# Interleaving GpSimd's loads with its copies for the later head pairs of a pooled-attention and feed-forward kernel

## The chip, the cores and the metric

The kernel runs on one core of one Trainium2 chip. The metric is device time in microseconds (us) of one execution. The profile comes from one further execution with the hardware profiler on.

The engines are named as the profile names them: PE is TensorE (matrix products; PEld is its weight load), DVE is VectorE, ACT is ScalarE, POOL is GpSimd, SP is SyncE. Each engine takes its instructions in the order in which they were written. SP only issues DMAs; POOL issues DMAs and also computes. All DMAs share 16 DMA engines.

## The reference

```
q_pool = mean of neighbouring query rows (1152 -> 576 rows)
attn   = softmax(q_pool @ k^T / sqrt(64))      # 8 batches x 8 heads
x      = (attn @ v), heads side by side         # 4608 x 512
out    = ((x @ w1) * (x @ w2)) @ w3 @ w_out     # 512 -> 1024 -> 1024 -> 512
```

Inputs and output are float32; products are made in 16-bit floats with 32-bit sums. The kernel folds `w3 @ w_out` into one matrix `T16` and leaves the maximum out of the softmax.

## The kernel before

**Tiling.** Two heads of a batch make a pair; there are `NP` = 32 pairs (four to a batch). A pair has 9 key tiles by 576 pooled query rows for each head. Scores are written in chunks of 512 columns for both heads at once, 10.125 chunks to a pair, 324 in all. For a chunk, PE writes scores to PSUM (L294, tile `psc`), ACT takes the exponential into a ring in SBUF (L300, `er`), and after a pair's last chunk two bursts of products with the values follow (`attend`, L312 and L321, `po`). DVE divides by the row sums (`xn`), and SP transposes the result by DMA into `xT` (L348), for every fourth remainder also `xR` (L330). When a batch is complete, its feed-forward products follow: `pg` (L514, against w1 and w2), the gate `gT` on DVE, `pp` (L535, against `T16`), and a store by SP.

**Order.** The main loop walks the chunks. A planner holds clocks of what PE, ACT and DVE would take and fills the time between chunks with products of earlier batches; whatever it emits stands in that order on PE for good. Preparation of a pair depends on `at`, the position in pairs (chunk times 512 over 5184), and does not enter the planner's clocks.

**Preparing pairs 9 to 31.** Pairs 0 to 8 are transposed on PE (`prep_pe`, queue `prep`). From `NPE` = 9 on, POOL copies the keys from their staging tile `kst` to `kc` (L161), adds neighbouring query rows from `qst` into `qp` (L143), and copies the values from `vst` into one of four tiles `vt` (L152). SP then transposes `kc` into `kT` (L166) and `qp` into `qT` (L172) by DMA. `prep_dma(P)` is called about 1.9 pairs ahead of pair P's scores and emits the three POOL operations at once. The SP parts are entries of the list `turns`, due 1.45 pairs (`turn_k`) and 1.2 pairs (`turn_q`) ahead. Behind the key transpose, `turn_k` puts a one-element copy `seen` on POOL (L168) that reads `kT`: POOL waits there until the transpose has landed. Only then come the loads from HBM of a pair five further on: keys L116, queries L108, and the values of pair P+4 (L123).

So POOL's cycle for a pair is: `seen`, three DMA issues, `kc`, `qp`, `vt`, and a wait at the next `seen`. SP's order for the same stretch mixes `kT` and `qT` with the transposes into `xT` and `xR` and the stores of finished rows (L600).

The buffers that matter: `kst` and `vst` have 5 each, `qst` 3 (each of two pairs, one in either half of the partitions), `kc` 2, `qp` 2 (each of two pairs), `kT` and `qT` 3, `vt` 4.

Of the kernel before, what the change touches and what calls it, by code (L numbers as in the profile page):

```python
# [8 lines left out]
FP16 = mybir.dt.float16  # L9
# [6 lines left out]
NJ = 9  # L16
# [7 lines left out]
def kernel(  # L24
# [11 lines left out]
    nc = tc.nc  # L36
    B, H, S, D = q.shape
# [5 lines left out]
    NP = B * H // 2  # L43
    SCL = 16.0
    NPE = 9
# [5 lines left out]
    ab = ctx.enter_context(tc.tile_pool(name="ab", bufs=4))  # L51
# [25 lines left out]
    kst, vst, qst, kT, qT, qps = {}, {}, {}, {}, {}, {}  # L77
# [25 lines left out]
    def load_q(P):  # L103
        if P % 2 == 0:
            qst[P // 2] = stage.tile([128, 2, 18, D], FP16, tag="qst", bufs=3, name="qst")
        b, h0 = P // 4, 2 * (P % 4)
        o = 64 * (P % 2)
        nc.gpsimd.dma_start(  # L108
            out=qst[P // 2][o:o + 64].rearrange("p u t d -> p u (t d)"),
            in_=q[b, h0:h0 + 2].rearrange("u (p t) d -> p u (t d)", t=18))  # L110

    def load_k(P):
        b, h0 = P // 4, 2 * (P % 4)
        kst[P] = stage.tile([128, 2, NJ, D], FP16, tag="kst", bufs=5, name="kst")
        for js in ((0, 3), (3, NJ)) if P == 0 else ((0, NJ),):
            nc.gpsimd.dma_start(  # L116
                out=kst[P][:, :, js[0]:js[1], :],
                in_=k[b, h0:h0 + 2].rearrange("u (p j) d -> p u j d", j=NJ)[:, :, js[0]:js[1], :])

    def load_v(P):  # L120
        b, h0 = P // 4, 2 * (P % 4)
        vst[P] = stage.tile([128, 2, NJ, D], FP16, tag="vst", bufs=5, name="vst")
        nc.gpsimd.dma_start(  # L123
            out=vst[P].rearrange("p u j d -> p u (j d)"),
            in_=v[b, h0:h0 + 2].rearrange("u (p j) d -> p u (j d)", j=NJ))

    def load(P):


        if P < NP:  # L130
            load_k(P)
            load_q(P)
        if P <= NP:
            load_v(P - 1)

    def pool_q(P, eng=None):

        pp, o = P // 2, 64 * (P % 2)
        if P % 2 == 0:
            qps[pp] = ab.tile([128, NJ, 2, D], FP16, tag="qp", bufs=2, name="qp")  # L140
        r = slice(o, o + 64)
        src = qst[pp][r].rearrange("p u (c two) d -> p u c two d", two=2)
        (eng or nc.vector).tensor_tensor(  # L143
            out=qps[pp][r].rearrange("p c u d -> p u c d"),
            in0=src[:, :, :, 0, :], in1=src[:, :, :, 1, :], op=ALU.add)

    def new_kq(P):
        kT[P] = ab.tile([128, NJ, 128], FP16, tag="kT", bufs=3, name="kT")
        qT[P] = ab.tile([128, NJ, 64], FP16, tag="qT", bufs=3, name="qT")

    def copy_v(P, eng=None):
        (eng or nc.vector).tensor_copy(out=vts[P % 4][:, :, :, 0:D], in_=vst.pop(P))  # L152

    turns = []

    def prep_dma(P):

        pp, o = P // 2, 64 * (P % 2)
        new_kq(P)
        kc = ab.tile([128, NJ, 2, D], FP16, tag="kc", bufs=2, name="kc")  # L160
        nc.gpsimd.tensor_copy(out=kc.rearrange("p j u d -> p u j d"), in_=kst.pop(P))  # L161
        pool_q(P, nc.gpsimd)
        copy_v(P, nc.gpsimd)

        def turn_k():
            nc.sync.dma_start_transpose(out=kT[P], in_=kc.rearrange("p j u d -> p (j u d)"))  # L166
            if P + 5 <= NP:
                nc.gpsimd.tensor_copy(out=seen[:, 0:1], in_=kT[P][0:1, 0, 0:1])  # L168
                load(P + 5)

        def turn_q():
            nc.sync.dma_start_transpose(  # L172
                out=qT[P], in_=qps[pp][o:o + 64].rearrange("p c u d -> p (c u d)"))
        turns.extend([(P - 1.45, turn_k), (P - 1.2, turn_q)])

    kcs, kc_done = {}, {}
# [126 lines left out]
    def attend(P, u):  # L303

        n = take()
        po = bank("po", n)
        for j in range(NJ):
            for i in range(4):  # L310
                r = ((P * NJ + j) * SQ) % RING + 128 * i
                nc.tensor.matmul(  # L312
                    po[:, VW * i:VW * i + D + 1], er[:, u, r:r + 128],
                    vts[P % 4][:, u, j, 0:D + 1],
                    start=(j == 0 and i == 0), stop=(j == NJ - 1 and i == 3),
                    skip_group_check=True)
        if u == 0:
            for j in range(NJ):
                r = ((P * NJ + j) * SQ) % RING + 512
                for s in range(2):  # L320
                    nc.tensor.matmul(  # L321
                        po[64 * s:64 * s + 64, 4 * VW:4 * VW + D + 1], er[:, s, r:r + 64],
                        vts[P % 4][:, s, j, 0:D + 1], start=False, stop=(j == NJ - 1),
                        skip_group_check=True)
        at = max(clock[0], clock[1], exp_done[last_chunk(P)] + T_SEM) + T_PV[u]
        clock[:] = [at] * 2
        give(n, normalize(P, u, po, 5 - u, at))
        b, hp = divmod(P, 4)
        if u == 0 and b % 2 == 1:
            nc.sync.dma_start_transpose(  # L330
                out=xR[:, hp, b // 2].rearrange("p u r -> p (u r)"),
                in_=rems[:, hp].rearrange("p s d -> p (s d)"))
        if u == 0 and hp == 3:
            ended.append((b, [vec + (8.0 if b < 2 else 6.5)]))
# [68 lines left out]
    def swap_due():  # L403
        half = 0 if swaps[0] else 1
        free = 3 if prep[0] or prep[1] else 2
        return bool(swaps[half]) and max(clock) > WEIGHTS[half] and len(spare) >= free and (
            spare[0][0] < min(clock))
# [29 lines left out]
    prep, ffn = ([], []), ([], [])  # L437
# [164 lines left out]
    def last_rows(places, lhsT):  # L602
# [24 lines left out]
        out=ident, in_=ident, compare_op=ALU.not_equal, fill=1.0,  # L627
# [49 lines left out]
    while c < NCHUNK or bursts or ffn[0] or ffn[1]:  # L677
        h = 0 if clock[0] <= clock[1] else 1
        if bursts and (c > bursts[0][0] or c == NCHUNK) and spare and spare[0][0] < clock[h] and (
                fresh or c > bursts[0][0] + 1 or c == NCHUNK):  # L680
            attend(*bursts.pop(0)[1:])
            fresh = False
            while swap_due():
                swap_halves()
            continue
        if c >= NCHUNK or due(c) > clock[h]:
            fresh = False
            if c >= NCHUNK and not tail and not bursts:
                tail = True
                spare += [(max(clock), 4), (max(clock), 5)]  # L690
            keep = 1 if prep[0] or prep[1] or bursts and c > bursts[0][0] - 1 else 0
            if not step(h):
                if swap_due():
                    clock[:] = [max(clock) + 0.1] * 2
                    swap_halves()
                    clock[:] = [clock[0] + 0.1] * 2
                else:
                    clock[h] += 0.02
            while ended and not early and not prep[0] and not prep[1]:
                b, ready = ended.pop(0)  # L700
                add_batch(b, ready)
            continue
        at = c * CH / PAIR
        scores(c, h)
        fresh = True
        for i in range(2):
            clock[i] += T_SC
        expo(c)
        exp_done.append(max(exp_done[-1] if c else 0.0, max(clock) + T_SEM) + T_EXP)
        if c == 0:  # L710
            prep_rest(rest)
        if jobs:
            n, job = jobs.pop(0)
            job()
            vector(n, 0.0)
        if staged < NPE and at >= STAGE.get(
                staged, staged - (0.95 if staged < 4 else 1.3)):
            prep_stage(staged)
            staged += 1
        while events and at >= events[0][0]:  # L720
            _, n, act = events.pop(0)
            act(n)
        todo = prepped < NP and at >= PREP.get(prepped, prepped - (
            0.65 if prepped < 4 else 0.9 if prepped < NPE else 1.9))
        if todo and prepped >= NPE:
            prep_dma(prepped)
            prepped += 1
        elif todo and prepped < staged and prepped in kcs:
            prep_pe(prepped)
            prepped += 1  # L730
        elif early and c >= early[0][0] and len(w3T) < 4:
            w3_transpose(early.pop(0)[1])
        while turns and at >= turns[0][0]:
            turns.pop(0)[1]()
        c += 1
    for emit, store, _, _ in last[:-1]:
# [36 lines left out]
```

## Time and profile before

| what | value |
|---|---|
| time, three runs | 420.18 us median (420.1, 420.18, 423.63) |
| the profiled execution | 425.27 us, of it span 423.3 us |
| granted clock of PE, mean | 0.995 |
| PE busy | 403.7 us (95%) |
| ACT busy | 331.1 us (78%) |
| DVE busy | 218.9 us (52%) |
| POOL busy | 191.2 us (45%) |
| DMA | 59.02 MB in 94219 packets |

The span runs from the first to the last instruction; 1.97 us of the profiled execution lie around it. PE's first product starts 6.0 us into the span and its last ends 3.9 us before the end. In rows of the timeline, the columns are start, duration (both us), engine, line, operation, output and inputs, shape, count, and in brackets the idle time before with what ended it. "issue" in that place stands for a wait on nothing that the profile shows.

### The profile page before, as it was taken

Reading aid. Unit: us, or ns where it says so; the run is one execution under the profiler, and the core shown is the slowest. Engines: PE = TensorE matmul, PEld = TensorE weight load, DVE = VectorE, ACT = ScalarE, POOL = GpSimd, SP = SyncE. Lnnn points to the kernel's source line nnn. Section 1 sums busy time; section 2 is a strip of 40 time slices with the busy share of each in tenths; the row PEclk is TensorE's granted clock in tenths of the full one; section 3 lists DMA queues with packets and bytes.
Section 4 is the critical chain, followed back from the end, with each engine's and each line's share of the span. In section 5 each row is a group of like instructions: output and inputs, shape, how many; then the busy total and the mean of one; then the engine's idle time right before and its main releaser. Section 6 shows DMA issues by size and latency. Waiting matters only on the chain.

```text
span 423.3 us, 17431 instructions
## 1 busy us (share of the span) xinstructions
PE 403.7 (95%) x7666; PEld 318.0 (75%) x7666; DVE 218.9 (52%) x596; ACT 331.1 (78%) x382; POOL 191.2 (45%) x209
## 2 busy tenths in 40 slices
PE   3799999998999999999999899999999999999996
PEld 1366665777768887888788786788878887888993
DVE  2266656875435653565365663356446644542540
ACT  3968888887788888888888788889888888834432
POOL 8233345860566576555655556665569300000000
PEclk9999999999899999999999999999999999999999
DMA  8999999999699999999999999999996215102004
GB/s 120 206 207 202 186 205 204 189 161 121 110 154 206 152 141 153 196 144 121 192 170 132 139 134 132 190 185 150 137 170 141 42 35 133 43 19 101 4 11 141
DMA packets 94219, 59.02 MB, mean 139 GB/s; under 512 B 64832, under 2 KB 84544, under 8 KB 94144
## 3 DMA queue, kind: packets, MB, share of 16 engines
q0 software_dynamic: 26528, 33.56, 50.7%
q1 hardware_dynamic: 67456, 24.22, 35.1%
q8 instruction: 60, 0.98, 1.0%
q10 hardware_dynamic: 160, 0.13, 0.1%
q14 instruction: 15, 0.12, 0.1%
HBM read 67.11 MB, written 9.44 MB: 181 GB/s over the span
## 4 chain that ended last, share of the span: by engine, by line
PE 93%; ACT 3%; issue 2%; DMA 1%; DVE 0%; POOL 0%; DVEq 0%; ACTq 0%; POOLq 0%
PE pg L514 30%; PE psc L294 19%; PE po L312 18%; PE pp L535 15%; PE pT L477 4%; PE po L321 3%; ACT er L300 3%; PE t L262 1%; PE sw L391 1%; DMA kst<-in_k_dram 1%; PE w3t L465 0%; PE pp L608 0%; PE tb L195 0%; POOL qst L108 0%; ACT kc L207 0%
## 5 line engine op out<-in xcount | busy, mean ns | idle before, releaser
L300 ACT ACTIVATE er<-psc 128x1024 f16<-128x1024 f32 x324 | 308.8, 1030 | 52.0 <-PE psc L294 48.7
L294 PE MATMUL psc<-qT,kT 64*128 64x384 f16 (+7 forms) x1152 | 132.3, 291 | 4.6 <-ACT er L300 3.8
L514 PE MATMUL pg<-xT,w2sb 64*128 64x256 f16 x1024 | 131.3, 270 | 0.0
L514 PE MATMUL pg<-xT,w1sb 64*128 64x256 f16 x1024 | 130.7, 271 | 0.1
L514 PEld LDWEIGHTS <-w1sb 64*128 64x128 f16 x1280 | 97.9, 94 | 10.9 <-issue 2.7
L514 PEld LDWEIGHTS <-w2sb 64*128 64x128 f16 x1280 | 96.7, 94 | 6.2 <-issue 0.4
L535 PE MATMUL pp<-T,gT 64*128 64x512 f16 (+1 forms) x552 | 94.4, 376 | 0.0
L312 PEld LDWEIGHTS <-er 128*128 128x128 f16 x2304 | 74.5, 98 | 17.6 <-issue 15.0
L294 PEld LDWEIGHTS <-kT 64*128 64x128 f16 x1152 | 60.6, 95 | 32.5 <-issue 16.8
L312 PE MATMUL po<-vt,er 128*128 128x65 f16 x2304 | 82.4, 194 | 2.0 <-issue 1.8
L506 DVE TENSOR_TENSOR gT<-pg,asb 128x256 f16<-128x256 f32 (+1 forms) x160 | 66.3, 417 | 20.8 <-ACT asb L494 16.3
L497 DVE COPY asb<-pg 128x256 f32<-128x256 f32 (+1 forms) x119 | 48.0, 404 | 32.1 <-PE pg L514 30.5
L340 DVE RECIPROCAL rz<-po 128x4 f32<-128x4 f32 x64 | 12.1, 189 | 89.7 <-PE po L312 46.0
L143 POOL TENSOR_TENSOR qp<-qst 64x1152 f16<-64x1152 f16 x23 | 54.5, 2370 | 1.0
L535 PEld LDWEIGHTS <-gT 64*128 64x128 f16 (+1 forms) x552 | 41.3, 94 | 13.8 <-issue 0.4
L168 POOL COPY seen<-kT 1x1 f16<-1x1 f16 x19 | 3.4, 180 | 88.0 <-DMA kT<-kc 88.0
L152 POOL COPY vt<-vst 128x1152 f16<-128x1152 f16 x28 | 32.1, 1150 | 4.6 <-issue 3.9
L123 POOL DMA_DIRECT2D vst<-in_v_dram x32 | 23.3, 729 | 17.2 <-DMA kst<-in_k_dram 7.4
L116 POOL DMA_DIRECT2D kst<-in_k_dram x33 | 24.0, 729 | 11.7 <-issue 3.0
L343 DVE TENSOR_TENSOR xn<-po,rz 128x256 f16<-128x256 f32 x64 | 27.2, 424 | 2.2
L494 ACT COPY asb<-pg 128x256 f32<-128x256 f32 (+1 forms) x41 | 12.8, 332 | 19.4 <-PE pg L514 18.9
L161 POOL COPY kc<-kst 128x1152 f16<-128x1152 f16 x23 | 26.9, 1169 | 0.0
(62 smaller groups left out, 256.2 us busy)
## 6 DMA issues: line engine op xcount, KB each, us to landing
qst<-in_q_dram POOLq DMA_DIRECT2D x32, 288.0 KB, 6.0
vst<-in_v_dram POOLq DMA_DIRECT2D x32, 288.0 KB, 8.2
kst<-in_k_dram POOLq DMA_DIRECT2D x31, 288.0 KB, 5.4
out_dram<-osb SPq DMA_DIRECT2D x32, 256.0 KB, 3.2
w3h<-in_moe_w_dram POOLq DMA_DIRECT2D x4, 512.0 KB, 15.6
wosb<-in_moe_w_out_dram POOLq DMA_DIRECT2D x1, 1024.0 KB, 13.8
xT<-xn SPq DMA_TRANSPOSE x64, 5.8
w1sb<-in_moe_w_dram POOLq DMA_DIRECT2D x2, 512.0 KB, 15.9
```

The lines of the kernel that those rows point to most:

```text
L116: nc.gpsimd.dma_start(out=kst[P][:, :, js[0]:js[1], :], in_=k[b, h0:h0 + 2].rearrange("u (p j) d -> p u j d", j=NJ)[:, :, js[0]:js[1], :])
L143: (eng or nc.vector).tensor_tensor(out=qps[pp][r].rearrange("p c u d -> p u c d"), in0=src[:, :, :, 0, :], in1=src[:, :, :, 1, :], op=ALU.add)
L152: (eng or nc.vector).tensor_copy(out=vts[P % 4][:, :, :, 0:D], in_=vst.pop(P))
L161: nc.gpsimd.tensor_copy(out=kc.rearrange("p j u d -> p u j d"), in_=kst.pop(P))
L294: nc.tensor.matmul(t[:, u, o:o + ln], kT[P][s, j, :], qv[s, f0:f0 + ln], start=True, stop=True)
L300: nc.scalar.activation(out=er[:, :, r:r + CH], in_=psc.pop(c), func=AF.Exp, bias=0.0, scale=SCALE)
L312: nc.tensor.matmul(po[:, VW * i:VW * i + D + 1], er[:, u, r:r + 128], vts[P % 4][:, u, j, 0:D + 1], start=(j == 0 and i == 0), stop=(j == ...
L343: nc.vector.tensor_tensor(out=xn, in0=acc[:, 0:4, 0:D], in1=rz[:, 0:4].to_broadcast([128, 4, D]), op=ALU.mult)
L497: nc.vector.tensor_copy(out=a, in_=t[:, 0:n])
L506: nc.vector.tensor_mul(out=g, in0=b, in1=a)
L514: nc.tensor.matmul(t[:, n * w:n * w + n], (w1sb, w2sb)[w][s, (m + h) % 2, m // 2, fs], x(s, m), start=start, stop=stop, skip_group_check=True)
L535: nc.tensor.matmul(t, gT[h][s, i, cs], T16[s, i, :], start=start, stop=stop, skip_group_check=True)
```

## The change

`prep_dma` no longer emits POOL's three operations together. A new function `copy_k` makes the key copy. `turn_k(P)` now emits, in this order: the SP transpose of pair P's keys, `seen`, the key load of P+5, the key copy of P+1, the query load of P+5, the query sums of P+1, the value load of P+4, and the value copy of P. Only for the first such pair (P = 9) do key copy and query sums stay in `prep_dma`. The buffers `kT` and `qT` are taken in `turn_k`. Turns now also wait until the planner's queue `prep` of PE transposes is empty.

```diff
-    def prep_dma(P):
-
-        pp, o = P // 2, 64 * (P % 2)
-        new_kq(P)
+    def copy_k(P):
         kc = ab.tile([128, NJ, 2, D], FP16, tag="kc", bufs=2, name="kc")
         nc.gpsimd.tensor_copy(out=kc.rearrange("p j u d -> p u j d"), in_=kst.pop(P))
-        pool_q(P, nc.gpsimd)
-        copy_v(P, nc.gpsimd)
+        kcs[P] = kc
+
+    def prep_dma(P):
 
         def turn_k():
-            nc.sync.dma_start_transpose(out=kT[P], in_=kc.rearrange("p j u d -> p (j u d)"))
+            new_kq(P)
+            nc.sync.dma_start_transpose(
+                out=kT[P], in_=kcs.pop(P).rearrange("p j u d -> p (j u d)"))
             if P + 5 <= NP:
                 nc.gpsimd.tensor_copy(out=seen[:, 0:1], in_=kT[P][0:1, 0, 0:1])
-                load(P + 5)
+            if P + 5 < NP:
+                load_k(P + 5)
+            if P + 1 < NP:
+                copy_k(P + 1)
+            if P + 5 < NP:
+                load_q(P + 5)
+            if P + 1 < NP:
+                pool_q(P + 1, nc.gpsimd)
+            if P + 5 <= NP:
+                load_v(P + 4)
+            copy_v(P, nc.gpsimd)
 
         def turn_q():
+            pp, o = P // 2, 64 * (P % 2)
             nc.sync.dma_start_transpose(
                 out=qT[P], in_=qps[pp][o:o + 64].rearrange("p c u d -> p (c u d)"))
+        if P == NPE:
+            copy_k(P)
+            pool_q(P, nc.gpsimd)
...
-        while turns and at >= turns[0][0]:
+        while turns and at >= turns[0][0] and not prep[0] and not prep[1]:
             turns.pop(0)[1]()
```

## The prediction

> **What bounds the kernel.** I read the page first (busy shares, then the chain that ended last), then the waits, then the rows of PE where it stands idle, then POOL's and SP's rows of one pair.
>
> ```profile
> PE 403.7 (95%) x7666; PEld 318.0 (75%) x7666; DVE 218.9 (52%) x596; ACT 331.1 (78%) x382; POOL 191.2 (45%) x209
> q8 instruction: 60, 0.98, 1.0%
> PE 93%; ACT 3%; issue 2%; DMA 1%; DVE 0%; POOL 0%; DVEq 0%; ACTq 0%; POOLq 0%
> ```
>
> PE is busy for 95% of the span and carries 93% of the chain; POOL, the engine that the change reorders, carries none of it. PE's idle time is 19.6 us: 6.0 before its first product, 3.9 behind its last, and 9.7 between. Pair 9, the first that the change touches, is prepared from about 90 us on, and 4.3 of those 9.7 lie before 25 us. After 90 us, PE's idle stretches over 0.3 us are three, all put down to "issue". The largest, in PE's timeline:
>
> ```profile
> 101.29 0.42 PE L312 MATMUL po<-vt,er 128*128 128x65 f16 x8
> 103.52 1.02 PE L312 MATMUL po<-vt,er 128*128 128x65 f16 x28 [1.81 <-issue]
> ```
>
> It stops in the middle of a burst whose inputs are there. The others are 0.68 us ending at 230.27 and 1.45 us ending at 242.09; a fourth delay, 0.53 us at 252.8, is seen only as a late start. What they share is a distance. The instruction queue (q8 above) moved 60 packets of 0.98/60 MB = 16 KB, and 2 x 7666 PE and PEld instructions over 60 are 256 a packet. Windows laid between the restarts (columns: window, its length, then each engine's busy time and count):
>
> ```profile
> 230.28:242.08 11.80, 10.36 (x256) 8.95 (x256) 6.54 (x21) 9.55 (x11) 6.91 (x7) 1.00 1.03 125
> 242.10:252.80 10.70, 10.44 (x256) 9.16 (x256) 6.73 (x22) 8.11 (x9) 6.80 (x7) 1.00 1.00 130
> ```
>
> 256 products and 256 weight loads are 512 instructions, exactly two packets; from 103.52 to 230.27 it is 4864, nineteen. PE runs dry at the edge of a block of its own instructions, because the next block's packet came late. The packets of that queue start up to 4.1 us after PE crosses the edge before: under 0.7 us where no load runs any more (after 322 us), 3 to 4 us where the DMA engines are full. This is the only door by which the change can reach PE's time.
>
> A stall can cost more than itself. After the one at 103.5 (columns as above, clock third from the end):
>
> ```profile
> 104.00:105.00 1.00, 1.00 (x26) 0.83 (x24) 0.38 (x2) 0.03 (x1) 0.18 (x1) 0.91 0.85 186
> 105.00:108.00 3.00, 3.00 (x32) 2.10 (x28) 1.10 (x3) 2.03 (x3) 2.96 (x4) 0.50 0.46 52
> ```
>
> Three and a half us at half clock lose about 1.8 us, so that stall cost 1.8 + 1.8 = 3.6 us. The stalls of 0.68 and 1.45 us cost no clock. The runs shown differ by 423.63 - 420.1 = 3.5 us, the same size: I take it that a run either has this event or not.
>
> **The change on POOL.** One cycle before, from POOL's timeline:
>
> ```profile
> 219.25 0.18 POOL L168 COPY seen<-kT 1x1 f16<-1x1 f16 x1 [4.75 <-DMA kT<-kc]
> 219.50 0.74 POOL L116 DMA_DIRECT2D kst<-in_k_dram  x1
> 220.23 0.61 POOL L108 DMA_DIRECT2D qst<-in_q_dram  x1
> 220.82 0.73 POOL L123 DMA_DIRECT2D vst<-in_v_dram  x1
> 221.54 1.18 POOL L161 COPY kc<-kst 128x1152 f16<-128x1152 f16 x1
> 222.65 2.39 POOL L143 TENSOR_TENSOR qp<-qst 64x1152 f16<-64x1152 f16 x1
> 224.97 1.15 POOL L152 COPY vt<-vst 128x1152 f16<-128x1152 f16 x1
> ```
>
> The work is the same seven instructions, 7.0 us a pair, none added: the cycle only becomes seen, k, kc, q, qp, v, vt. Counted from `seen`: the key copy ends at 0.25 + 0.74 + 1.18 = 2.2 us, not 3.5 (1.3 earlier); the query load issues at 2.2, not 1.0; the query sums end at 5.2, not 5.8; the value load issues at 5.2, not 1.6; the value copy ends at 7.0 as before, but is that of pair P, not P+1. The whole fits: POOL waits 88 us at `seen` over 19 pairs, 4.6 us each.
>
> **On SP.** `kT` waits for `kc`, and everything behind it on SP waits along:
>
> ```profile
> SPq L166 <- POOL kc L161: 20.9, 8, 4.9
> ```
>
> (total, times, longest) and in SP's timeline:
>
> ```profile
> 222.74 1.94 SPq L166 DMA_TRANSPOSE kT<-kc  x1
> 224.77 1.52 SPq L348 DMA_TRANSPOSE xT<-xn  x1
> 226.38 1.69 SPq L172 DMA_TRANSPOSE qT<-qp  x1
> ```
>
> Here `kT` of pair 20 was due on SP when the chunk of 220.0 us was written, and started when the copy ended, 222.7. Behind it stood `xT`, whose `xn` was ready at 222.2. From `seen` to the next `seen` is 11.4 us here: 3.5 to `kT`'s issue and 7.9 until it lands, because the three loads fill the DMA engines from 221 to 227 (their queue's packets take a share of about 1.0, the transposes' queue moves nothing from 221 to 225). With 1.3 us less the cycle is near 10.1 us, below the 10.85 us that PE takes for a plain pair, so the lag does not pile up, and `kT`, `xT` and `qT` go up to 2.7 us earlier in pairs 11 to 13, 19 to 21 and 26 to 28.
>
> What does PE gain from that? Nothing directly. Each `kT` already lands 3.0 to 11.5 us before the first score product that reads it, each `qT` 1.2 (pair 25) to 9.1 us; no wait of PE names either. An `xT` is first read 0.8 us (fourth batch, landing 206.0, read 206.8) to 28 us after its batch's last one lands. **Sum on the path: 0.** If that cover went, each pair would cost PE what it is late.
>
> The other edits: `vt` of pair P now ends about 7 us after `seen(P)`, near the start of P's scores; the products that read it start over a pair (10.85 us) later: 0. Taking `kT` later (at 1.45 instead of 1.9 pairs) changes nothing, as the pair whose buffer it takes had its last scores at 2.0: 0. The empty-queue condition can hold only pair 9's turn: PE's last transposes (L262) run until 97.1 us and that turn's chunk is at 96.7, so one chunk, 1.1 us, and SP reaches that `kT` only at 99.7, behind `xR`; it lands 9.6 us early: 0.
>
> **What is left: the instruction packets.** Stalls after 104 us are 0.68 + 1.45 + 0.53 = 2.66 us, in the stretch 217 to 253 where the short products of the remainder rows make PE cross a block in 5 to 7 us. The three packets behind them waited 3.1, 3.3 and 3.4 us while `kT`, `xT` and `qT` ran together. Packets that met a load burst waited as long (3.7 us at 165.9, 3.9 at 267.7), but in longer blocks, without a stall. The stall at 101.7 stands before the first moved load (105.0): unchanged. So the change parts the loads, which cost nothing now, and moves the transposes, which do, by 1 to 2.7 us, which may help or hurt. Bounds: all three go, -2.66; or one grows to the size of that at 101.7, clock included, +3.6. I take the smallest of the three gone, -0.5, as the shift is small against the 7 us of a transpose. The profiled execution becomes 425.27 - 0.5 = 424.8; against the median, which is 5.1 lower (3.6 for the event at 101.7, the rest smaller stalls without the profiler, I suppose), 420.18 - 0.5 = **419.7 us**.
>
> [...]
>
> **Rivals.**
> - *All three stalls go*, because spread loads leave the DMA queues shallower: 420.18 - 2.66 = 417.5. For it: the waits under 0.7 us where no loads run. Against: those three packets stood behind transposes. Chance 0.12. More than 1% (below 416.0) would need gains where PE shows no gap: 0.04 on top.
> - *Slower: a late packet with the clock drop.* The value load now issues at 5.2 us and runs on until about 9, so the DMA engines have no quiet stretch before the next `kT`; a packet asked for then waits 4 us, and in a 5 us block PE stops. It decides from about 1.8 us of stall on, the size that cost clock. One such event is +3.6 (423.8), chance 0.09; two, 427.4, chance 0.06. Against: the total traffic is the same.
> - *Slower: late tiles.* The value load, issued 3.6 us later, pushes back the transposes behind it. The least covered are `qT` of pairs 25, 26 and 27 (1.2, 2.9, 2.5 us) and the fourth batch's last `xT` (0.8). If all landed 3 us later, PE would lose 1.8 + 0.1 + 0.5 + 2.2 = 4.6, 424.8: chance 0.05, half of it over 1%. Against: the loads' work is the same, and the first two of a cycle are out of the way sooner.
> - *SP held by `qp`.* For even P, `turn_q(P)` now comes after the sums of P+1, in the other half of the same tile. If the wait covered the tile, `qT` would start 5.2 us after `kT` landed, land some 4.5 later, 9.7 in all against a cover of about 6: 3.7 us late in the 9 even pairs up to 26: +33, 453. Against: SP writes parts of `xT` while PE reads others, without a wait. Chance 0.03.
> - *It doesn't do what it says*: `kc` still stands behind `seen`, so SP's wait shrinks by 1.3 us a pair only and the phases hardly move: 420.2. This lies inside the forecast's case, which has 0.61 in all.
>
> **Chances and range.** About 1% (4.2 us) is what a measurement of this kernel can tell from no change. Faster: 0.04. Slower: 0.06 + 0.03 + 0.03 = 0.12. Same: 0.84. The range goes from all stalls gone, 417.5, to one event with the clock, 424.0.
>
> **What would show it.** POOL rows in the new order, `kc` ending 2.2 us after `seen`; SP's wait for `kc` well below 20.9 us; `seen` no longer over 11 us apart in 207 to 243; POOL's 88 us at `seen` still there; PE's rows in the same order, its stalls still at edges 256 instructions apart, that at 101.7 untouched. I am wrong if PE waits for `kT`, `qT` or `xT`, or if half-clock stretches appear between 110 and 300 us.

## The result, and the profile after

| | before | after |
|---|---|---|
| median of 20 runs | 422.71 us (420.08 to 424.95) | 426.60 us (421.72 to 433.29) |
| ratio | 1 | 1.0091, 95% interval 1.0067 to 1.0116 |
| profiled execution, span | 425.27, 423.3 us | 428.29, 426.4 us |

The change made the kernel slower by 0.9%; 419.7 us had been forecast, with no difference that a measurement can tell. 2.5 of the 6.9 us of that miss are the base: the three runs of before that were shown had a median of 420.18, twenty have 422.71. The other 4.4 are the effect, 3.9 slower where 0.5 faster was forecast. All ratios in this document leave out runs over 1.5% above the fastest of the same kernel, here five of the twenty after, and among these is the run whose trace follows (428.29 us).

The trace of before is of 425.27 us, above all its twenty times. What the two traces show is one pair of executions, 3.0 us apart.

The page after, its busy shares and the chain that ended last by engine and by line:

```profile
PE 403.7 (95%) x7666; PEld 317.2 (74%) x7666; DVE 220.3 (52%) x596; ACT 332.1 (78%) x382; POOL 190.2 (45%) x209
...
PE 75%; DMA 12%; POOL 5%; ACT 3%; issue 2%; DVE 1%; SPq 0%; POOLq 0%; DVEq 0%; ACTq 0%
PE pg L530 25%; PE psc L310 15%; PE po L328 15%; PE pp L551 11%; DMA kT<-kc 7%; PE pT L493 4%; DMA qT<-qp 4%; POOL qp L143 3%; ACT er L316 3%; PE po L337 2%; PE t L278 1%; POOL kc L158 1%; DMA kst<-in_k_dram 1%; PE sw L407 1%; POOL qst L108 1%
```

PE is busy for the same 403.7 us. But the chain, 93% PE before, now leaves PE for a fifth of the span: it runs through `kT`'s and `qT`'s transposes and through POOL's `qp` and `kc`. The preparation of pairs has become part of the bound. The orders of instructions on PE, DVE, ACT and SP are the same in both programs; only POOL's differs.

Of PE's waits (who waited for what: us in total, times, longest):

```profile
PE pg L530 <- issue: 4.8, 5, 1.3
...
PE psc L310 <- DMA qT<-qp: 2.1, 3, 1.6
```

No wait of PE named `qT` before. In PE's timeline, one stall of either kind:

```profile
191.19 0.27 PE L530 MATMUL pg<-xT,w2sb 64*128 64x256 f16 x1 [1.27 <-issue]
...
307.28 0.34 PE L310 MATMUL psc<-qT,kT 64*128 64x384 f16 x2 [1.58 <-DMA qT<-qp]
```

The first lies at an edge of 256 instructions, as those of before did: PE crossed the edge before at 183.8 us, and the next packet of its instructions started only at 187.9, 4.2 us later.

As PE's order is the same, product n of one trace can be laid beside product n of the other. Up to 127 us the changed kernel gains 3.1 us, nearly all because the stall at 101.7 us (1.81 us) and the half clock behind it (3.4 us, from 104.8 to 108.2) are missing: after, the granted clock is 1.00 there. From there to the end it loses 6.1: 3.2 net at edges of instruction blocks (the largest +1.38 at 177 us and +1.45 at 191) and 2.7 at score products that wait for `qT` (0.35, 0.57 and 1.79, in pairs 18, 25 and 26).

POOL's rows of one long cycle:

```profile
161.47 0.18 POOL L170 COPY seen<-kT 1x1 f16<-1x1 f16 x1 [6.03 <-DMA kT<-kc]
161.98 0.72 POOL L116 DMA_DIRECT2D kst<-in_k_dram  x1 [0.33 <-issue]
162.70 1.16 POOL L158 COPY kc<-kst 128x1152 f16<-128x1152 f16 x1
163.79 0.60 POOL L108 DMA_DIRECT2D qst<-in_q_dram  x1
164.45 2.35 POOL L143 TENSOR_TENSOR qp<-qst 64x1152 f16<-64x1152 f16 x1
166.75 0.74 POOL L123 DMA_DIRECT2D vst<-in_v_dram  x1
167.54 1.14 POOL L152 COPY vt<-vst 128x1152 f16<-128x1152 f16 x1
176.83 0.18 POOL L170 COPY seen<-kT 1x1 f16<-1x1 f16 x1 [8.14 <-DMA kT<-kc]
```

and SP's rows of the key transposes:

```profile
166.68 1.34 SPq L167 DMA_TRANSPOSE kT<-kc  x1
...
178.96 2.36 SPq L167 DMA_TRANSPOSE kT<-kc  x1
```

The order and the times behind `seen` are the forecast ones: key copy done after 2.4 us, value load out at 5.3, value copy done at 7.2. But the cycle takes 15.4 us, not 10.1. `kT` is issued at 166.68 and the value load at 166.75. `kT` lands at 176.8, after 10.1 us, where the longest before was 8.3; the values land at 175.1, after 8.4, which is within the 6.1 to 9.3 of before. The next two cycles take 9.5 and 14.6 us, the last again with a `kT` of 9.7 us and the value load 0.4 us behind it. At the next `seen`, so late, key load, key copy and query load follow, and the next `kT`, due at 174.5 us and reached by SP at 177.6, waits for its copy until 178.96.

DMA times from issue to landing, as the view of each tile gives them (us, smallest, median, largest):

| | before | after |
|---|---|---|
| `kT` | 3.3, 5.5, 8.3 | 3.3, 6.8, 10.1 |
| `qT` | 2.7, 4.5, 6.1 | 2.7, 5.5, 9.1 |
| DMA share, 104 to 315 us | 1.02 (155 GB/s) | 1.12 (153 GB/s) |

The DMA engines are busier with the same bytes (59.02 MB in either trace). That alone is not the loss: two variants below that lose nothing (0.9995 and 0.9975) have a share of 1.11. The cover of `qT` ahead of its first score product, 1.2 us at the least before, is 0.3 or less in pairs 16, 18, 19, 25 and 26.

These are two spells, not one. After the slow cycles the cover is back at 7.0 us in pair 22, and then it goes again, with no `kT` over 7.3 us: SP takes 4.9 us to issue the `kT` of pair 23 (1.5 before), and those of pairs 24 to 26 are issued 2.5 to 3.0 us later than before, where PE is 0.7 behind. In pair 26 the value load is issued 0.1 us ahead of `qT`, and `qT` takes 8.2 us (5.5 before). Rows of SP for pairs 23 and 26, and of POOL:

```profile
260.93 4.86 SPq L167 DMA_TRANSPOSE kT<-kc  x1
...
296.16 2.12 SPq L167 DMA_TRANSPOSE kT<-kc  x1
299.07 1.24 SPq L185 DMA_TRANSPOSE qT<-qp  x1
```

```profile
298.99 0.74 POOL L123 DMA_DIRECT2D vst<-in_v_dram  x1
```

2.4 of the 2.7 us of waits for `qT` are in this second spell. Why SP fell behind there the rows do not say.

### The profile page after: what moved, and what is told of

It reads as the page before. It is cut to its first block, busy times and chain, and to the rows that moved or that the text cites. A ratio compares the mean times of both kernels' runs of the same rounds, so it can differ in the third digit from the quotient of the medians.

```text
span 426.4 us, 17439 instructions
## 1 busy us (share of the span) xinstructions
PE 403.7 (95%) x7666; PEld 317.2 (74%) x7666; DVE 220.3 (52%) x596; ACT 332.1 (78%) x382; POOL 190.2 (45%) x209
## 2 busy tenths in 40 slices
DMA packets 94219, 59.02 MB, mean 138 GB/s; under 512 B 64832, under 2 KB 84544, under 8 KB 94144
## 4 chain that ended last, share of the span: by engine, by line
PE 75%; DMA 12%; POOL 5%; ACT 3%; issue 2%; DVE 1%; SPq 0%; POOLq 0%; DVEq 0%; ACTq 0%
PE pg L530 25%; PE psc L310 15%; PE po L328 15%; PE pp L551 11%; DMA kT<-kc 7%; PE pT L493 4%; DMA qT<-qp 4%; POOL qp L143 3%; ACT er L316 3%; PE po L337 2%; PE t L278 1%; POOL kc L158 1%; DMA kst<-in_k_dram 1%; PE sw L407 1%; POOL qst L108 1%
## 5 line engine op out<-in xcount | busy, mean ns | idle before, releaser
L522 DVE TENSOR_TENSOR gT<-pg,asb 128x256 f16<-128x256 f32 (+1 forms) x160 | 66.3, 417 | 20.9 <-ACT asb L510 16.3
L510 ACT COPY asb<-pg 128x256 f32<-128x256 f32 (+1 forms) x41 | 12.8, 332 | 19.4 <-PE pg L530 18.9
```

The costliest lines, as they stand in the source:

```text
L522: nc.vector.tensor_mul(out=g, in0=b, in1=a)
```

## First experiments: which part of the change

All edits are to the changed kernel, inside `turn_k`; `seen` comes first unless shown. Theory A said that the longer the loads stretch, the worse; theory B that the earlier key copy does the harm; theory C that any new order falls out by chance.

**Loads together.**

```diff
             if P + 5 < NP:
                 load_k(P + 5)
-            if P + 1 < NP:
-                copy_k(P + 1)
             if P + 5 < NP:
                 load_q(P + 5)
-            if P + 1 < NP:
-                pool_q(P + 1, nc.gpsimd)
             if P + 5 <= NP:
                 load_v(P + 4)
+            if P + 1 < NP:
+                copy_k(P + 1)
+            if P + 1 < NP:
+                pool_q(P + 1, nc.gpsimd)
             copy_v(P, nc.gpsimd)
```

> The changed kernel with its three loads back to back again behind seen, the copies of the next pair behind them; the other parts of the change (copies one turn ahead, buffers taken in the turn, the empty-queue condition) stay. Theory A (crowding: parted loads run for 10 instead of 6 us of each cycle and the transposes get through only between them): ratio to the kernel before 1.000, within 0.003, and kT and qT land after medians near 5.6 and 4.8 us, as before, not 7.0 and 6.5. Theory B (the key copy, 1.3 us earlier, sends the transposes into the loads): 1.000 as well, since the copy ends 3.5 us behind seen again. Theory C (any new order shifts the instruction packets by chance): anything from 0.995 to 1.010. If it stays at 1.009, neither A nor B holds and one of the other parts of the change is the cause.

Measured: ratio 0.9958, interval 0.9929 to 0.9988; `kT` 3.2, 6.7, 8.7 us and `qT` 2.7, 5.0, 6.6. The loss is gone, so, theory C apart, it lies in the order of loads and copies. `kT`'s median did not come back (6.7, not 5.6); its largest nearly did. It is faster than before by a little more than was allowed for. Against before this program only copies the values a pair later, and for the last pairs in another place.

**Only the value load parted.**

```diff
-            if P + 1 < NP:
-                copy_k(P + 1)
             if P + 5 < NP:
                 load_q(P + 5)
             if P + 1 < NP:
+                copy_k(P + 1)
                 pool_q(P + 1, nc.gpsimd)
```

> Key and query load together behind seen, then key copy, query sums, value load, value copy: only the value load is parted from the others. Theory A: the value load, issued about 5 us behind seen, falls together with the next kT, so most of the loss is here: 1.005 to 1.009, qT landing after 6 us or more. Theory B: the key copy ends 2.8 instead of 3.5 us behind seen, half of the shift, so about 1.004. Theory C: 0.995 to 1.010.

Measured: 0.9995 (0.9957 to 1.0033). A fails: the loads stretch almost as in the changed kernel, and nothing is lost. B's 1.004 lies just outside the interval.

**Value load moved up to the query load.**

```diff
             if P + 5 < NP:
                 load_q(P + 5)
+            if P + 5 <= NP:
+                load_v(P + 4)
             if P + 1 < NP:
                 pool_q(P + 1, nc.gpsimd)
-            if P + 5 <= NP:
-                load_v(P + 4)
```

> Key load, key copy, then query and value load together, then query sums and value copy: the key copy ends 2.2 us behind seen as in the changed kernel, the loads are all out by 3.5 us instead of 6. Theory A: the loads stay nearly in one run, 1.000 to 1.004. Theory B: the key copy is as early as in the changed kernel, so the whole loss, 1.009. Theory C: 0.995 to 1.010.

Measured: 1.0696 (1.0634 to 1.0758), from three runs with a median of 451.92 us. No theory expected this: the loads stretch less than in the changed kernel, and over seven times as much is lost. POOL's and SP's rows of a cycle, and the chain by line:

```profile
222.31 0.60 POOL L108 DMA_DIRECT2D qst<-in_q_dram  x1
222.90 0.72 POOL L123 DMA_DIRECT2D vst<-in_v_dram  x1
223.69 2.36 POOL L143 TENSOR_TENSOR qp<-qst 64x1152 f16<-64x1152 f16 x1
226.11 1.15 POOL L152 COPY vt<-vst 128x1152 f16<-128x1152 f16 x1
233.93 0.18 POOL L170 COPY seen<-kT 1x1 f16<-1x1 f16 x1 [6.67 <-DMA kT<-kc]
```

```profile
222.41 2.09 SPq L167 DMA_TRANSPOSE kT<-kc  x1
```

```profile
DMA kT<-kc 31%; PE pg L530 14%; PE psc L310 8%; PE po L328 8%; PE pp L551 6%; DMA qT<-qp 4%; POOL kc L158 4%; PE pT L493 4%; ACT er L316 2%; POOL qp L143 2%; POOL kst L116 1%; PE po L337 1%; PE t L278 1%; POOL vst L123 1%; PE sw L407 1%
```

The end of the key copy releases `kT` on SP and the two loads on POOL in the same half microsecond. `kT` then takes 11.5 us, and the cycle repeats it: 13.0 us on average, against the 10.85 that PE takes for a pair. 31% of the chain is that one transpose. PE's waits from 60 to 345 us come to 22 us, 14.8 of them for `qT`. Around the longest of them its granted clock is 0.50 for 23.9 us in all; PE is busy for 18.4 us of these; half of that, about 9 us, is my estimate of what the clock cost it.

How much the DMA engines wrote meanwhile does not mark such a collision. While this `kT` was under way, from 222.4 to 233.9 us, loads and the SP queue together wrote 119 KB a us. But before, the same measure is between 124 and 207 for the nineteen `kT` issued from 104 to 315 us, and the three slow `kT` of the changed kernel have 186, 116 and 132.

**Copies ahead of `seen`,** all three loads behind it:

```diff
+            if P + 1 < NP:
+                copy_k(P + 1)
+            if P + 1 < NP:
+                pool_q(P + 1, nc.gpsimd)
+            copy_v(P, nc.gpsimd)
             if P + 5 <= NP:
                 nc.gpsimd.tensor_copy(out=seen[:, 0:1], in_=kT[P][0:1, 0, 0:1])
...
             if P + 5 < NP:
                 load_k(P + 5)
             if P + 5 < NP:
                 load_q(P + 5)
             if P + 5 <= NP:
                 load_v(P + 4)
```

> Key copy, query sums and value copy ahead of seen, in the time in which POOL idles 4.6 us a pair, and the three loads together behind it: SP never waits for a copy, and the loads stay in one run. Theory A: 0.997 to 1.001, qT landing near 4.8 us, SP's wait for kc under 2 us in total. Theory B: the transposes go earliest of all, so at least 1.009. Theory C: 0.995 to 1.010.

Measured: 1.0014 (0.9980 to 1.0049). B is out: the copies are earliest of all, and the time is that of before. It gains nothing either. SP's wait for `kc` is 6.0 us, and three `kT` took 10.4 to 10.9 us: each was issued between the query load and the value load of a burst, the value load 0.1 to 0.8 us behind it. This trace is of a run of 429.71 us, the longest of the twelve, so how often the others met such `kT` is not known.

## The new theory: a load issued just behind a transpose

Theory D, a guess at the mechanism: a `kT` that SP issues while POOL has still a load to issue shares the engines with it, and both are slow (in the variant of 1.0696 `kT` took 9.2 to 11.6 us, the value load 8.8 to 11.1); one issued behind the last load waits for the loads, and then has the engines (before, `kT` took 3.3 to 8.3 us).

**Query load last.**

```diff
             if P + 5 < NP:
                 load_k(P + 5)
+            if P + 5 <= NP:
+                load_v(P + 4)
             if P + 1 < NP:
                 copy_k(P + 1)
...
-            if P + 5 <= NP:
-                load_v(P + 4)
             copy_v(P, nc.gpsimd)
```

> Order on GpSimd: seen, key load, value load, key copy, query load, query sums, value copy. As many loads are parted by the key copy as in the changed kernel, and all are out by 3.5 us behind seen, as in the slow variant with key load, key copy, query and value load. New theory D (collision: a key transpose that SP issues while POOL still has a load to issue within the next 1.5 us shares the DMA engines with that load packet by packet, and both take about 10 us instead of 6 to 7; a transpose issued once the last load is out waits for the loads and then runs alone): here only the query load, half as many partitions and out within 0.6 us, goes together with the transpose, and nothing comes behind it: kT lands in 6 to 8 us, ratio 1.000, within 0.006. Theory A (parting in itself costs): about the same as the slow variant, over 1.03.

Measured: 1.0030 (0.9992 to 1.0067); `kT` at most 8.7 us. A load that was parted in the same way, with none coming behind the transpose, cost little or nothing here.

**Value load at the key copy.**

```diff
-            if P + 1 < NP:
-                copy_k(P + 1)
             if P + 5 < NP:
                 load_q(P + 5)
             if P + 1 < NP:
-                pool_q(P + 1, nc.gpsimd)
+                copy_k(P + 1)
             if P + 5 <= NP:
                 load_v(P + 4)
+            if P + 1 < NP:
+                pool_q(P + 1, nc.gpsimd)
```

> Order on GpSimd: seen, key load, query load, key copy, value load, query sums, value copy. Against the variant with the value load behind the query sums, which measured 0.9995, the value load only goes ahead of the query sums: 2.4 us earlier, so that it is issued at the moment at which the key copy releases SP's kT, and the loads stretch less. Theory D (collision of a load with a transpose issued in the same 1.5 us): kT lands after 9 to 11 us, cycles of seen grow to 12.5 us and more, ratio 1.02 to 1.07. Theory A (the longer the loads stretch, the worse): at most the time of that variant, 0.995 to 1.002.

Measured: 1.0049 (1.0014 to 1.0085): slower, but by less than D asked. The traces say why in part: the value load came 0.1 us ahead of `kT`, not behind it, and `kT` took 7.7 to 9.2 us in such cycles.

**A half microsecond of filler** between key copy and value load puts the load behind the transpose:

```diff
             if P + 1 < NP:
                 copy_k(P + 1)
+            nc.gpsimd.tensor_copy(out=pad[:, 0:448], in_=wosb[:, 0, 0:448])
             if P + 5 <= NP:
                 load_v(P + 4)
```

(against the variant just before; `pad` is a new tile that nothing reads)

> Order on GpSimd: seen, key load, query load, key copy, a filler copy of 448 columns (about 0.5 us, its result is not used), value load, query sums, value copy. So far kT took 6.6 to 7.4 us where the value load was issued 2 to 2.9 us behind it, 9.7 to 11.6 where it came 0.1 to 1.5 us behind it, and 8 to 9.2 where it came 0.1 us ahead. Theory D (a load issued within 1.5 us behind a key transpose shares the engines with it): the filler moves the value load from 0.1 us ahead to about 0.4 us behind kT, so kT takes 10 to 11.5 us in the pairs whose kT waits for the key copy, cycles of seen are 13 us and more there, and the ratio is 1.03 to 1.07. Rival E (it takes two loads at the transpose, query and value, as in the slow variant): 1.005, as without the filler, plus at most 0.003 for half a us more on POOL.

Measured: 1.0108 (1.0072 to 1.0144), twice the loss of the same program without the filler, though the two intervals overlap. The direction is D's; the size is neither D's (1.03 at the least) nor E's (1.008 at the most). Of the seven `kT` with the value load 0.2 to 0.4 us behind, three took 9.7 to 11.1 us and four 7.4 to 8.2. So rival E has a part: with query load and value load both at the transpose, as in the variant of 1.0696, nearly every one was slow (9.2 to 11.6 us). After 104 us, PE waits for no tile in this trace; its stalls there, 3.8 us, are all "issue".

**Filler in the slow variant** (the edit is shown against the variant of 1.0696), between query and value load:

```diff
             if P + 5 < NP:
                 load_q(P + 5)
+            for n in (512, 512, 512):
+                nc.gpsimd.tensor_copy(out=pad[:, 0:n], in_=wosb[:, 0, 0:n])
             if P + 5 <= NP:
                 load_v(P + 4)
```

> The slow variant (1.0696: seen, key load, key copy, query load, value load, query sums, value copy) with three filler copies of 512 columns (about 1.6 us together, result not used) between query and value load: the value load goes from 0.5 us behind kT to about 2.2 us behind it, and all later work on POOL is 1.6 us later. Theory D: kT lands in about 7 us again, ratio 0.998 to 1.012. Theory A (the longer the loads stretch, the worse): not below 1.05. Rival E (query load at the transpose is enough together with any value load behind it): about 1.07.

Measured: 1.0106 (1.0070 to 1.0141). 2 us of useless work on POOL win back 5.9 of 7 points. Where the value load came 2.4 us behind `kT`, it took 6.6 to 8.4 us; of three cycles in which `kT` was issued later, and met the load at 0.4, 1.3 and 0.8 us, two still gave 11.5 and 10.8, and the third 5.9.

**Filler in the changed kernel itself:**

```diff
             if P + 1 < NP:
                 pool_q(P + 1, nc.gpsimd)
+            for n in (512, 512, 512, 512):
+                nc.gpsimd.tensor_copy(out=pad[:, 0:n], in_=wosb[:, 0, 0:n])
             if P + 5 <= NP:
                 load_v(P + 4)
```

> The changed kernel with four filler copies of 512 columns (about 2.1 us together, result not used) between query sums and value load, which is then issued about 7.4 instead of 5.2 us behind seen; the loads stretch more, and POOL has 2 us less to spare. In the changed kernel kT of pairs 12, 15 and 17, issued about 5 us behind seen, met the value load within 1.5 us and took 10 us each. Theory D: these now have the value load 2 us behind them, no kT over 9 us, ratio 0.997 to 1.004. Theory A: at least 1.009, as the changed kernel or worse.

Measured: 0.9975 (0.9947 to 1.0003): the whole loss is gone, with every part of the change kept and more work on POOL. Rows of POOL and of SP for the cycle that took 15.4 us above:

```profile
162.57 2.35 POOL L144 TENSOR_TENSOR qp<-qst 64x1152 f16<-64x1152 f16 x1
164.99 2.65 POOL L181 COPY pad<-wosb 128x512 f16<-128x512 f16 x4
167.58 0.74 POOL L124 DMA_DIRECT2D vst<-in_v_dram  x1
```

```profile
166.88 1.80 SPq L168 DMA_TRANSPOSE kT<-kc  x1
```

The value load is now 0.7 us behind this `kT`, closer than meant, and it still took 8.1 us, not 10; once more a load came 0.6 us behind (that `kT` took 4.7 us), elsewhere 1.3 us or more. The largest `kT` is 8.7 us. The chain is PE's again:

```profile
PE 92%; DMA 2%; ACT 2%; DVE 2%; issue 1%; POOL 1%; DVEq 0%; ACTq 0%; POOLq 0%
```

**All traces together.** In the fourteen traces of this study, the `kT` issued between 104 and 315 us, by the loads around them:

| loads around the issue of `kT` | count | median us | over 9.4 us |
|---|---|---|---|
| two or more in the 4 us ahead, another within 1.5 us behind | 27 | 10.4 | 18 |
| all others | 235 | 6.8 | 5 |

The bounds (4, 1.5 and 9.4 us) were fitted to these same traces, and nine of the 18 are in the variant of 1.0696. Before has no `kT` in the first row: there the key copy stood behind the three loads, so whatever it released came 1.9 us or more after the last of them. The changed kernel has one, which took 10.1 us. Its other two slow ones, the 10.1 and the 9.7 us above, had a single load in the 4 us ahead and count among the five of the second row: the rule of the table does not catch them.

The same traces speak to theory C. Nearly every single ratio lies in its range, 0.995 to 1.010, or a hair above it, so none but 1.0696 excludes chance by itself. But the programs fall into two sets by the number of `kT` over 9.4 us in their traces:

| `kT` over 9.4 us | programs, by ratio |
|---|---|
| 2 to 10 | 1.0091 (three), 1.0696 (ten), 1.0108 (three), 1.0106 (two), 1.0107 (two; see below), and 1.0014 (three, the copies ahead) |
| none | 0.9958, 0.9975, 0.9984, 0.9995, 1.0030, 1.0035, 1.0049, and before |

Orders that fell out by chance would not sort like this. With one trace for each program it stays an argument, and the copies ahead are against it.

## Two checks

**Loads together, once more.** The kernel of the first experiment, with no edit to it.

> The first experiment's kernel once more (three loads together behind seen, value copy a pair later than before; measured 0.9958, interval 0.9929 to 0.9988). If it is faster than the kernel before, again below 1.000 with its whole interval; if that was chance, an interval around 1.000.

Measured: 0.9984 (0.9957 to 1.0012). The gain over before is at most some tenths of a per cent, and not sure.

**SP's turns earlier,** in the changed kernel and in the one with loads together:

```diff
-        turns.extend([(P - 1.45, turn_k), (P - 1.2, turn_q)])
+        turns.extend([(P - 1.8, turn_k), (P - 1.55, turn_q)])
```

> The changed kernel with both SP turns 0.35 pairs (3.8 us) earlier: turn_k at 1.8 and turn_q at 1.55 pairs ahead of the scores instead of 1.45 and 1.2; the order on GpSimd stays, and since seen moves along, the value load still meets kT. In the changed kernel's trace, aligned product by product with the kernel before, PE lost 2.7 us to qT that came late and 3.2 us to instruction packets. If these are two prices: qT is no longer late, the packets still are, ratio 1.003 to 1.006, kT still at 10 us in some pairs. If the late qT is the whole price: 0.997 to 1.002. If the earlier transposes change nothing: 1.009.

> The variant with three loads together behind seen (0.9958 and 0.9984 in two studies) with both SP turns 0.35 pairs earlier. No tile is late there without this, so theory D forecasts no gain: 0.995 to 1.001, kT in 5 to 8 us. If PE still waits on tiles in runs without the profiler, it is faster: below 0.995.

Measured: 1.0107 (1.0061 to 1.0153) and 1.0035 (1.0012 to 1.0057). Neither is as expected. In the first, every `qT` lands 2.5 us or more ahead of its products and PE waits for none, yet the loss is as large as without the edit, and two `kT` still take 10.3 and 12.0 us. The largest of PE's waits behind its first one, at the start, in the view of waits:

```profile
PE pg L530 <- issue: 3.9, 4, 2.1
```

So a loss of this size needs no late `qT`. In this trace PE's stalls from 60 to 345 us come to 4.9 us, all of them "issue"; in those of the variants that lose nothing (0.9958, 0.9975, 0.9984 and 0.9995) all stalls come to 1.3 to 2.2. The one trace of before has 4.2, but it is of a longer run than any of its twenty. That the packets come late because of the slow `kT` is not shown. The second program shows that earlier turns cost 0.5 to 0.8 points by themselves, with no `kT` over 8.8 us. Its trace has an `xT` that PE waits 1.9 us for, but this is the longest of its twelve runs (428.09 us). The difference of the two programs is still 0.7 points. How the loss of the changed kernel divides between late `qT` and late packets over many runs stays open; one trace says 2.7 and 3.2 us.

## Why the prediction was wrong

- **That POOL's work, its order and its times behind `seen` would be as worked out** was right to 0.2 us. SP's wait for `kc` fell from 20.9 us to 12.8, less than meant.
- **"With 1.3 us less the cycle is near 10.1 us"** is the step that failed, and with it **"Sum on the path: 0"**, which rested on it. It took the 7.9 us from `kT`'s issue to its landing as fixed, or shorter with fewer loads ahead. In the traces they went with what was issued just behind: in the changed kernel `kT` took 9.7 to 10.1 us in three of the four cases in which the value load came up to 1.5 us behind it (3.6 in the fourth, the last of the loads), and cycles of 13.6, 15.4 and 14.6 us stand between 125 and 201 us. Where `kT` went out as soon as its copy ended, as the forecast had in mind, the step held: four cycles from 201 to 239 us took 8.7 to 10.4 us. Over all, a cycle took 11.5 us on average, as before. That the place of the value load is what costs is best shown by the filler ahead of it (0.9975 where the changed kernel had 1.0091). The forecast had both numbers needed: the value load at 5.2 us behind `seen`, and `kT` due 10.85 us behind the one before, which lands about 5.5 us after its issue. That puts the two at the same moment.
- **"The only door"**: instruction packets were a door, and 3.2 us went through it. Packets of before started anywhere up to 4.0 us behind the edges between 104 and 315 us, not 3 to 4 throughout; after, up to 5.1. But the covers of 1.2 to 9.1 us ahead of the scores, called enough, were used up twice, within four slow cycles by pair 18 and again in pairs 25 and 26, and PE waited for `qT`, a second door. The prediction had named that as a sign of being wrong. The second spell, with most of the wait, had no slow `kT`; its cause stays open.
- **The rival "a late packet with the clock drop"** named the value load and the longer stretch of loads, and came nearest, but had the wrong price: no clock drop is in the trace after (granted clock 1.000), and a longer stretch in itself cost nothing here (0.9995 with nearly as long a one and 0.9975 with a longer one). Nor did the clock turn on about 1.8 us of stall: the 1.81 us of before were followed by 3.4 us at half clock, but 2.09 us (turns earlier, at 238.5; mean granted clock of that run 1.000) and 2.26 us (half a microsecond of filler, at 233.2) were not. The rival "late tiles" gave 424.8 us and the right tile, and two of its three pairs, 25 and 26, waited; its chance was put at 0.05, on the argument that the loads' work is the same. The bytes are, and from 104 to 315 us the engines moved nearly as many a microsecond (153 against 155); but the transfers took other times: `qT` 4.8 us at the median of that stretch before, 6.5 after.
- **The rival "SP held by `qp`"** did not happen: in every even pair up to 26 `qT` was issued before the sums of the next pair had begun. What did hold `qT`, by 0.5 to 0.9 us in pairs 16, 18 and 26, were the sums of its own pair.
- **The stall at 101.7 us, "unchanged"**: it is in none of the thirteen traces behind the first. All of these programs copy pair 9's values later. Whether that is the reason isn't known; there is one trace of before. Nor do the twenty times of before, spread evenly from 420 to 425 us, fall into two groups 3.5 us apart, as I took three of them to do.
- **The median of three runs as the base** was 2.5 us low.

## What to carry to other kernels

Before parting a burst of DMAs, work out where each part falls against the other queue's transfers, in a cycle that includes the gate (`seen` here): in the variant of 1.0696 two waits released by one event put `kT` and the value load 0.5 us apart at 222.4 us and again at 236.1, and the chain gated by that `kT` kept the collision going (cycles of 13.0 us on average, against the 10.85 of PE). Treat a transfer's time to landing as a price that can change with its neighbours (`kT`: 3.3 to 8.3 us before, up to 13.3 in that variant), not as a row to be copied over. And where an engine's cover is a few microseconds, ask how many cycles of a slower chain it lasts (that of `qT` was gone here within four).

## What was not expected of the hardware

A transpose within SBUF and two loads from HBM that were issued within 0.6 us slowed each other: in the variant of 1.0696 the transpose took 9.2 to 11.6 us and the value load 8.8 to 11.1, where before they took 3.3 to 8.3 and 6.1 to 9.3. The time of the transpose went with the order of issue to within a microsecond: value load 0.1 us ahead of it, 7.7 to 9.2 us (the variant of 1.0049); 0.5 us behind with the query load at its side, 9.2 to 11.6; about 2 us or more behind, at most 8.8 in all but two. These two, at 1.9 and 2.0 us, took 10.3 and 12.0 us, both in the variant with the earlier turns. A value load within a microsecond behind is not enough by itself: it also stands beside transposes of 3.6 us (the changed kernel, at 314.0), 4.7 (the same with its filler) and 5.9 (the slow variant with its filler). What happens inside the DMA engines no trace here shows.
